# First 1024 tokens of a retention-plus-MLP kernel as 256-token pairs of sessions with a block-diagonal state product, and product 1's token sums on GpSimd

## The chip, the cores and the metric

One core of a Trainium2 chip. The metric is the device time of one execution in microseconds (us), the median over several executions.

The engines are named as in the profile: PE is TensorE's matmul side, PEld its weight loads, DVE is VectorE, ACT is ScalarE, POOL is GpSimd. "Bank" means one PSUM bank of 128 partitions by 512 fp32 columns.

## The reference

The reference is retention (a linear attention with decay, 8 batches, 8 heads, 576 positions, 64 per head) followed by an MLP on 4608 tokens with 512 inputs and 2048 hidden units, whose gate is h cos h:

```python
scores = scale * np.matmul(q, k.transpose(0, 1, 3, 2))
gamma = 1.0 - 2.0 ** (-5.0 - np.arange(H, dtype=np.float32))
Dmat = np.where(rel >= 0, gamma[:, None, None] ** rel[None, :, :], 0.0)
ret = scores * Dmat[None, :, :, :]
attn = np.matmul(ret, v)
# ... heads put side by side: x is (4608, 512)
h = x @ w_in                 # 512 -> 2048
g = h * np.cos(h)
out = g @ w_out              # 2048 -> 512
```

## The kernel before

The program lists its operations with the data that each reads and writes. When it is built, a list scheduler with a cost for each operation puts them in one fixed order per engine and gives each a PSUM bank.

Retention is computed in chunks with a running state. The first 1024 tokens go in 128-token sessions (token pairs share a partition), the rest in smaller pieces. One session does the scores, their mask, the product with the state so far (inter), the state update and the product with V (intra):

```python
def big_s(self, g):
    boxes, x, pt = [Box(), Box()], SES[g][0], self.PT[g % self.NPT]
    ...
    self.P.add("pe", mm, r=self.kkeys(g), w=boxes, cost=0.24 + 0.19)      # scores
    for hp in range(2):
        self.P.add("dve", mask(hp), r=boxes + ["trb"], ...)               # mask 128x512
```

V is scaled on 128 partitions and must then be shifted to the partitions where the session wants it:

```python
SHIFT = ('act', 'dve')
# cast_v, for the first eight tiles
for x in range(2):
    self.copy(SHIFT[x], ap(self.NAT[na], 2 * DM, 64 * x, 64, DM, [1, DM]),
              self.vt(t)[p0:p0 + 64, x * DM:(x + 1) * DM],
              [("sv", vb, x), ("sv", vb)], [("nat", na, 1, x)], DM, 0.75)
```

The state is copied from PSUM into a block-diagonal tile (two heads on the diagonal) by two 64-partition copies:

```python
for hp, eng in enumerate(engs):
    self.move(eng, lambda hp=hp: (
        ap(self.SBD[g % self.NSB], 1024, 64 * hp, 64, u0 * 512 + 64 * hp, [512, m], [128, 4], [1, 64]),
        ap(self.ST, 1024, 64 * hp, 64, u0 * 512, [512, m], [64, 4], [1, 64])), ...)
```

The first projection (mlp1) is a matmul group of 512 columns in one bank, a cosine on ACT, and on DVE the product of the two, which frees the bank and is called "the gt eviction" below:

```python
self.P.add("pe", mm, r=[("win", f // 2) for f in fs] + xts, w=[box], ...)
self.P.add("act", lambda e: e.activation(ap(cb, ...), self.bk(box.i, 0, 128, 0, m), AF.Sin, ...), ...)
self.P.add("dve", lambda e: e.tensor_tensor(ap(gt, ...), self.half_bank(box.i, ...), ap(cb, ...), ALU.mult), ...)
```

The second projection uses seven Strassen products per 512-token block. They need sums of gt halves ("token sums") and of w_out quarters ("weight sums"). All token sums are on DVE before the change. The sum for product 1 is

```python
self.P.add("dve", lambda e: e.tensor_tensor(
    ap(self.S1, HF * HB, 0, 128, f * HB, [HB, 2], [1, HB]), half(0, 0), half(1, 1), ALU.add), ...,
    cost=0.36, port=True, lazy=True)      # lazy: the scheduler takes it when nothing else is ready
```

## Time and profile before

| | before |
|---|---|
| time, median of 3 runs | 301.75 us (301.29 to 302.21) |
| span in the trace | 300.8 us |
| first useful projection matmul | 20.44 us |
| 8th, 16th, 24th gt eviction ended | 33.20, 42.77, 54.25 us |
| first Strassen product | 94.09 us |
| last matmul ended, last instruction ended | 297.75, 300.83 us |

How to read it: the span runs from the first to the last instruction. A line of a group has line number, engine, operation, output and inputs with their shapes, count, then busy time and mean ns of one, then the idle time just before them and who ended it. A line of waits has the engine and its output, who it waited for, then us in total, times and the longest. The lines themselves are in the prediction.

Two milestones: the first product, before which the front of the kernel lies, and the last matmul.

### The profile page before, as it was taken

The numbers are of one execution on the slowest core, as the hardware profiler recorded it, in microseconds if no ns is written. First come the engines' busy times: TensorE is split into PE (matmuls) and PEld (weight loads), VectorE is DVE, ScalarE is ACT, GpSimd is POOL, SyncE is SP. The second block draws the span as 40 slices with busy tenths as digits, with TensorE's granted clock in tenths as the row PEclk, the third lists the DMA queues.
The fourth block names the chain that finished last, engine by engine and source line by source line (L and its number), as shares of the span: only waits on it lengthen the run. The fifth ranks groups of instructions, "written<-read, shape, count | busy, mean of one in ns | idle before, by whom it ended". The sixth has DMA issues, their size and how long they took to land.

```text
span 300.8 us, 8802 instructions
## 1 busy us (share of the span) xinstructions
PE 288.0 (96%) x3659; PEld 206.2 (69%) x3695; DVE 239.5 (80%) x384; ACT 197.7 (66%) x340; POOL 143.7 (48%) x141
## 2 busy tenths in 40 slices
PE   8879899999999999999899999999999999999995
PEld 3457668765688885767576666676766676666684
DVE  5899889997899599679966985798589839964961
ACT  6467889946787556776667776766676767545420
POOL 4422950899854498088408941794050014002313
DMA  7999999899999999799859996999212011202023
GB/s 199 290 347 318 281 182 213 203 241 223 247 194 173 223 245 231 170 188 193 183 134 218 216 199 164 226 208 160 56 35 72 2 42 33 61 11 70 16 91 105
DMA packets 123894, 50.11 MB, mean 167 GB/s; under 512 B 82384, under 2 KB 123344, under 8 KB 123856
## 3 DMA queue, kind: packets, MB, share of 16 engines
q1 hardware_dynamic: 121744, 47.46, 74.4%
q0 software_dynamic: 2112, 2.10, 4.4%
q8 instruction: 29, 0.48, 0.7%
q14 instruction: 9, 0.07, 0.1%
HBM read 36.70 MB, written 9.44 MB: 153 GB/s over the span
## 4 chain that ended last, share of the span: by engine, by line
PE 80%; ACT 5%; DVE 4%; SPq 4%; DMA 3%; issue 2%; POOLq 0%; POOL 0%; DVEq 0%
PE bk L809 37%; PE bk L926 31%; PE bk L834 4%; DMA gt<-in_moe_w_in_dram 3%; ACT cb L817 2%; SPq L426 2%; PE st L640 2%; PE bk L619 2%; DVE gt L820 2%; PE bk L610 1%; PE bk L629 1%; SPq L445 1%; PE bk L567 1%; ACT xt L676 1%; ACT win L484 1%
## 5 line engine op out<-in xcount | busy, mean ns | idle before, releaser
L809 PE MATMUL bk<-xt,win 128*128 128x512 bf16 (+2 forms) x788 | 133.7, 314 | 4.2 <-DVE gt L820 1.0
L820 DVE TENSOR_TENSOR gt<-bk,cb 128x512 bf16<-128x512 f32 x144 | 95.9, 685 | 37.4 <-ACT cb L817 36.1
L817 ACT ACTIVATE cb<-bk,cpi 128x512 bf16<-128x512 f32 x144 | 97.8, 687 | 42.0 <-PE bk L809 37.3
L809 PEld LDWEIGHTS bk<-xt,win 128*128 128x128 bf16 x816 | 72.8, 98 | 41.1 <-ACT win L484 0.9
L961 POOL TENSOR_TENSOR sv<-sv,os 128x512 f32<-128x512 f32 x16 | 21.0, 1315 | 87.9 <-ACT os L970 66.7
L532 POOL TENSOR_TENSOR qnat<-qstg,wt 128x512 bf16<-128x512 f32 x34 | 38.9, 1164 | 19.2 <-DMA qstg<-in_q_dram 18.2
L676 ACT ACTIVATE sbd<-st 64x512 bf16<-64x512 f32 (+1 forms) x64 | 36.5, 570 | 15.0 <-PE bk L610 13.6
L487 POOL CAST nat<-stg 128x512 bf16<-128x512 f32 x36 | 27.3, 767 | 26.5 <-DMA stg<-in_k_dram 26.5
L522 POOL TENSOR_TENSOR nat<-stg,wt 128x512 bf16<-128x512 f32 x28 | 35.5, 1267 | 3.9 <-DMA stg<-in_v_dram 3.9
L926 PE MATMUL bk<-wout,gt 128*128 128x256 bf16 x256 | 31.7, 273 | 0.0
L926 PE MATMUL bk<-wout,s 128*128 128x256 bf16 x256 | 31.3, 273 | 0.3 <-DVE s L888 0.3
L926 PE MATMUL bk<-tw,gt 128*128 128x256 bf16 x256 | 31.3, 273 | 0.0
L676 ACT ACTIVATE xt<-bk 128x256 bf16<-128x256 f32 (+1 forms) x64 | 27.3, 488 | 5.4 <-DVE pt L655 3.8
L888 DVE TENSOR_TENSOR s<-gt 128x1024 bf16<-128x1024 bf16 x32 | 28.8, 902 | 1.4 <-PE bk L926 1.2
L926 PEld LDWEIGHTS bk<-wout,gt 128*128 128x128 bf16 x256 | 25.0, 98 | 6.1
L926 PEld LDWEIGHTS bk<-wout,s 128*128 128x128 bf16 x256 | 24.5, 98 | 6.4 <-DVE s L888 0.8
L895 DVE TENSOR_TENSOR gt<-gt 128x1024 bf16<-128x1024 bf16 x32 | 28.1, 881 | 0.0
L926 PEld LDWEIGHTS bk<-tw,gt 128*128 128x128 bf16 x256 | 24.0, 98 | 5.3 <-ACT sv L965 1.0
L655 DVE TENSOR_TENSOR pt<-bk,tri 128x512 bf16<-128x512 f32 (+2 forms) x30 | 19.8, 663 | 3.8 <-PE bk L610 3.7
L892 DVE TENSOR_TENSOR s<-gt 128x512 bf16<-128x512 bf16 x32 | 21.3, 664 | 0.0
L961 POOL TENSOR_TENSOR sv<-sv 128x512 f32<-128x512 f32 x8 | 13.2, 1656 | 15.5 <-ACT sv L965 10.3
L970 ACT ACTIVATE os<-bk 128x512 f32<-128x512 f32 x16 | 9.6, 597 | 13.0 <-PE bk L926 12.9
(75 smaller groups left out, 273.5 us busy)
## 6 DMA issues: line engine op xcount, KB each, us to landing
out_dram<-os SPq DMA_DIRECT2D x31, 256.0 KB, 2.4
qstg<-in_q_dram SPq DMA_DIRECT2D x12, 512.0 KB, 5.8
stg<-in_k_dram SPq DMA_DIRECT2D x24, 256.0 KB, 4.4
stg<-in_v_dram SPq DMA_DIRECT2D x24, 256.0 KB, 5.4
stg<-in_k_dram SPq DMA_DIRECT2D x4, 512.0 KB, 7.2
stg<-in_v_dram SPq DMA_DIRECT2D x4, 512.0 KB, 7.4
gt<-in_moe_w_in_dram SPq DMA_DIRECT2D x4, 512.0 KB, 8.5
wout<-in_moe_w_out_dram POOLq DMA_DIRECT2D x4, 512.0 KB, 10.8
```

What stands on the lines that cost most here:

```text
L487: self.P.add(eng, lambda e: e.tensor_copy(dst, src), r=r, w=w, cost=cost, port=eng == "pool")
L522: self.P.add(eng, lambda e: e.tensor_tensor(ap(self.NAT[na], 2 * DM, 0, 128, DM, [D, H], [1, D]), ap(self.STG[st], 2 * DM, 0, 128, DM, [D, ...
L532: self.P.add(eng, lambda e, x=x: e.tensor_tensor(ap(self.QNAT[slot], 2 * DM, 0, 128, x * DM, [D, H], [1, D]), ap(self.QSTG[slot], 2 * DM, ...
L676: self.P.add(eng, (lambda e: e.activation(*io(), AF.Copy)) if eng == "act" else (lambda e: e.tensor_copy(*io())), r=r, w=w, cost=0.127 + 0 ...
L809: inst = e.matmul(self.bk(box.i, 0, 128, i * n, n), ap(self.WIN, 4 * DFF, 0, 128, c * DFF + 128 * f, [1, 128]), ap(self.XT, 4 * XR, 0, 128 ...
L817: self.P.add("act", lambda e: e.activation(ap(cb, TB, 0, 128, 0, [1, m]), self.bk(box.i, 0, 128, 0, m), AF.Sin, bias=self.CPI.ap(), scale= ...
L820: self.P.add("dve", lambda e: e.tensor_tensor(ap(gt, NF * TB, 0, 128, f0 * TB + lo - TB * j, [TB, len(fs)], [1, n]), self.half_bank(box.i, ...
L888: self.P.add("dve", lambda e: e.tensor_tensor(ap(self.S5, HF * TB, 0, 128, f * TB, [1, 2 * TB]), ap(gt, NF * TB, 0, 128, f * TB, [1, 2 * TB]),
L892: self.P.add("dve", lambda e: e.tensor_tensor(ap(self.S1, HF * HB, 0, 128, f * HB, [HB, 2], [1, HB]), half(0, 0), half(1, 1), ALU.add), r= ...
L895: self.P.add("dve", lambda e: e.tensor_tensor(ap(gt, NF * TB, 0, 128, f * TB + HB, [HF * TB - HB, 2], [TB, 2], [1, HB]), ap(gt, NF * TB, 0 ...
L926: inst = e.matmul(self.bk(box.i, 0, 128, at * HB, HB), ap(lt, lsize, 0, 128, loff + f * lstep + 128 * t, [1, 128]), ap(rt, rsize, 0, 128, ...
L961: self.P.add(eng, lambda e: e.tensor_tensor(out(), a(), b(), op), r=r, w=w, cost=1.04 if eng == "pool" else 0.09 + 0.00104 * n * HB, port= ...
```

## The change

The intent: handle two sessions (256 tokens) together, so that V needs no shift, K is transposed and evicted for a pair at once, and the state is masked into its block-diagonal form by a single 128x512 product with a mask BD. With ACT relieved in the front, projections are woven through attention from the third unit on. In the later blocks, GpSimd adds the token sums of product 1. The last products are also re-ordered and held back differently. The diff, cut:

```diff
-HOLD = (2, 4)
-LS = (0, 1, 2, 3, 4, 5)
+HOLD = (1, 4)
+LS = (0, 1, 4, 2, 3, 5)
-EO, ES, EQ = ('act', 'act'), ('dve', 'dve'), ('pool', 'dve')
-WP = (7, 7, 7, 7, 8, 7, 7, 10)
-WC = ("dve", "act", "act", "dve", "pool", "dve", "dve", "act")
-G1, G2, WG = 3, 5, ("stg", 1, 1, 0)
-EARLY = 12
+EO, ES, EQ = ('act', 'act'), ('dve', 'act'), ('dve', 'pool')
+WP = (6, 5, 7, 8, 6, 9, 10, 9)
+WC = ("pool", "act", "act", "pool", "pool", "act", "act", "dve")
+G1, G2, WG = 3, 4, ("stg", 1, 1, 0)
+EARLY = 2
-SHIFT = ('act', 'dve')
-UNITS = ((0, 256, (0, 12)), (256, 512, (0, 12)), (0, 512, (12, 16)))
+UNITS = ((0, 256, (0, 10)), (256, 512, (0, 10)), (0, 512, (10, 16)))
+POOLED = 4
 ... (cast_v: the shift copies)
-            for x in range(2):
-                self.copy(SHIFT[x], ap(self.NAT[na], 2 * DM, 64 * x, 64, DM, [1, DM]),
-                          self.vt(t)[p0:p0 + 64, x * DM:(x + 1) * DM],
-                          [("sv", vb, x), ("sv", vb)], [("nat", na, 1, x)], DM, 0.75)
 ... (step_tk: one transpose group and one eviction of 128x1024 per pair; ev_st: one masked product)
+            self.P.add("dve", lambda e: e.tensor_tensor(
+                ap(self.SBD[g % self.NSB], 1024, 0, 128, u0 * 512, [128, 4], [64, 2], [1, 64]),
+                ap(self.ST, 1024, 0, 128, u0 * 512, [64, 4], [0, 2], [1, 64]),
+                ap(self.BD, 128, 0, 128, 0, [0, 4], [64, 2], [1, 64]), ALU.mult), ...)
 ... (big_s, big: scores, masks and intra products for two sessions at once, in 64-row tiles)
 ... (token_sums)
-        self.P.add("dve", lambda e: e.tensor_tensor(
+        eng = "pool" if j >= POOLED else "dve"
+        self.P.add(eng, lambda e: e.tensor_tensor(
             ap(self.S1, HF * HB, 0, 128, f * HB, [HB, 2], [1, HB]), half(0, 0), half(1, 1), ALU.add),
 ... (schedule)
-        run([m1(lo, hi, *fs) for lo, hi, fs in units[EARLY:]], [lambda: T(need[0])] + att_of(need[0], req(640)))
+        run([m1(lo, hi, *fs) for lo, hi, fs in units[EARLY:]], [lambda: T(need[0])] + att_of(need[0], need[0] + 2))
-        run([m1(512, 640, *f) for f in fours], att_of(req(640), req(768)))
-        run([m1(640, 768, *f) for f in fours], att_of(req(768), need[1]))
+        run([m1(512, 768, f, f + 1) for f in range(0, 16, 2)], att_of(need[0] + 2, need[1]))
```

WP spaces the loads of w_in among the other loads, WC says which engine casts each of its eight pieces, EARLY is the number of projection units issued ahead of any weaving, UNITS their shapes. LS is the order of the last products, HOLD how many products are held back, EO, ES and EQ the engines of some of attention's copies. A sum that moves to GpSimd also loses its `lazy` mark.

## The prediction

> **What bounds the kernel now.** I read the summary of the page first, then busy times by stage, then the tensor engine's waits in the stage that looked loose, then the groups that the change touches, and last the end of the chain. The summary and the slices of 7.5 us:
>
> ```profile
> PE 288.0 (96%) x3659; PEld 206.2 (69%) x3695; DVE 239.5 (80%) x384; ACT 197.7 (66%) x340; POOL 143.7 (48%) x141
> ...
> PE   8879899999999999999899999999999999999995
> ...
> DVE  5899889997899599679966985798589839964961
> ```
>
> TensorE (PE) bounds most of the span. 96% is no proof alone: a busy PE may run small matmuls badly. So I took the starts of successive matmuls in the timeline. From 94 us on, 128x512 matmuls follow each other every 216 ns and 128x256 ones every 109 ns, one moving column per 0.42 ns in both, and the weight loads (98 ns) hide. That pace does not improve; only holes can go. The table by stage (columns: window, its length, then busy us of PE, PEld, DVE, ACT, POOL) shows where they are:
>
> ```profile
> 20.40:54.50 34.10, 31.80 (x465) 25.15 (x468) 31.52 (x52) 29.26 (x47) 15.83 (x18) 1.00 1.13 252
> 54.50:94.30 39.80, 39.22 (x582) 29.54 (x585) 35.51 (x48) 29.72 (x55) 30.98 (x30) 1.00 1.10 219
> 94.30:294.30 200.00, 196.74 (x2427) 140.31 (x2453) 155.32 (x234) 127.40 (x222) 85.29 (x74) 1.00 0.67 133
> ```
>
> The first row runs from the first useful projection matmul to the moment when all projections of the first 768 tokens are issued. Counted by columns at full pace, its useful PE work is about 25 us of 34: some 9 us are holes or thin sequences. DVE is 92% and ACT 86% busy there, GpSimd only 46%. In the third row PE has 3.3 us of holes in 200 us. So the stage from 20 to 54 us is bound by evictions, by DVE before ACT, and by chains between them; the rest by PE. PE's waits from 18 to 62 us say whom it waits for:
>
> ```profile
> PE bk L695 <- DVE qt L541: 1.5, 2, 1.0
> PE bk L809 <- DVE gt L820: 0.6, 2, 0.4
> PE bk L809 <- ACT win L484: 0.6, 1, 0.6
> PE bk L809 <- DVE win L487: 0.4, 1, 0.4
> ```
>
> Each is an engine that was late because of its queue, none a DMA directly.
>
> **What the Trainium skill says.** "VectorE: DVE Perf Modes", section "The perf-mode tier table", gives a two-tensor operation with a PSUM operand the 1x rate and a copy from PSUM at most 2x. The trace agrees: 512 fp32 columns from PSUM take 685 ns in the cosine product, 1024 bf16 columns copied from PSUM 686 ns (groups below). Hence a masked product of 128x512 is not cheap. "SBUF — State Buffer", section "Who interferes with whom", says that a DVE instruction with two SBUF inputs contends with GpSimd reads, and one with a single SBUF input outside the two-port modes does not. The trace agrees sharply: the token sum that the change moves takes 407 to 1495 ns, the PSUM product 673 to 693 ns. "GPSIMD Engine Reference", section "Elementwise — side-by-side cycle accounting", has GpSimd 1.96 times slower than DVE on a two-tensor add; here its bf16-giving 128x512 product takes about 1.05 us (V scaling) against 0.41 undisturbed for the DVE sum. "TensorEngine Tiling (Array Packing)", section "PSUM Bottleneck", warns that after tiling the PSUM copies may become the bottleneck. That is this stage.
>
> ```profile
> L820 DVE TENSOR_TENSOR gt<-bk,cb 128x512 bf16<-128x512 f32 x144 | 95.9, 685 | 37.4 <-ACT cb L817 36.1 <-PE bk L610 0.5
> L892 DVE TENSOR_TENSOR s<-gt 128x512 bf16<-128x512 bf16 x32 | 21.3, 664 | 0.0
> L540 ACT ACTIVATE kt<-bk 128x512 bf16<-128x512 bf16 x14 | 8.1, 594 | 3.3 <-PE bk L549 3.2
> L541 DVE COPY qt<-bk 128x1024 bf16<-128x1024 bf16 x8 | 5.5, 686 | 1.0 <-PE bk L567 0.9
> L484 ACT ACTIVATE nat<-sv 64x512 bf16<-64x512 bf16 x8 | 5.0, 625 | 3.9 <-DVE sv L511 3.8
> L487 DVE COPY nat<-sv 64x512 bf16<-64x512 bf16 x8 | 3.6, 450 | 0.2
> L676 DVE CAST sbd<-st 64x256 bf16<-64x256 f32 x8 | 3.3, 418 | 0.2
> L676 ACT ACTIVATE sbd<-st 64x256 bf16<-64x256 f32 x6 | 2.2, 371 | 0.1
> ```
>
> **The change part by part, first 1024 tokens.** *PE work*: per 256 tokens the scores go from 16 matmuls of 64x128 to 32 of 64x64, and the intra products likewise from 16 to 32. Before two such tiles share the array, after four do, so the columns streamed per time stay equal: 8 x 56 ns = 0.45 us each, as the 16 score matmuls show now (0.62 us from first start to last end, with 0.17 of latency). I take zero change. The 512-to-768 projections become 64 matmuls at 109 ns in place of 128 at 56 ns: 0.2 us less.
>
> *Removed*: the V shifts, 8 x 0.625 = 5.0 us of ACT and 8 x 0.450 = 3.6 us of DVE; the half-size state copies, 3.3 us of DVE and 2.2 of ACT; eight K evictions of ACT, 4.8 us. *Added*: seven masked state products of 0.61 to 0.69 us on DVE, 4.5 us; four paired K evictions, 4 x 0.69 = 2.7 us of DVE. V scaling (4 DVE operations, 3.2 us) and two more weight casts go to GpSimd; three DVE weight casts vanish, ACT gets one more and the early K casts.
>
> For the stage 20.4 to 54.5 alone, by what falls in it: DVE loses 1.8 (shifts), 1.5 (state) and about 1.5 (casts), and gains five masked products, 3.0, and two K evictions, 1.4: a net of -0.4. It also contains 1.5 us of weight sums that need not be there. Its compulsory work is thus 31.5 - 1.5 - 0.4 = 29.6 us, an estimate. ACT goes from 29.3 to about 25. So ACT leaves the bound, while DVE hardly sheds work; what improves is the chain. Session 3 now finishes 6 us after the scores of its pair because state copy, inter product, state and intra follow one another per session; after, the scores of 256 tokens are masked at once and the intra products need no shift. The new load order also brings the second pair of sessions' inputs two loads earlier (some 1.9 us each), and attention is woven through the projections from the third unit on.
>
> The first projection can start when its weights are cast: they stay eighth in the queue, and a GpSimd cast no longer waits behind four DVE masks; I allow 0.8 us. From 19.6, 29.6 us of DVE without a hole gives 49.2; a little over 1 us of holes gives 50.3. That is 4.2 us before the 54.5 of now.
>
> *Next stage (54.5 to 94.3)*: the 1.5 us of weight sums return, and six more K evictions move from ACT to DVE at about 0.4 us (half of the 686 ns copy and some start cost), 2.4 us. DVE would go from 35.5 to 39.4 of 39.8 us. It can't hide wholly: I add 0.8 us.
>
> *Token sums*: 20 of the 32 sums go to GpSimd, 20 x 0.66 = 13.3 us off DVE. But PE waits only once for a token sum after 120 us, 0.3 us, with a hole near 206 us that a late DVE queue caused. I give 0.5 us, no more: DVE's idle time in a PE-bound stage costs nothing.
>
> *End*: the last matmul is at 297.75 and the result leaves DVE 0.6 us later. The chain shows GpSimd in between:
>
> ```profile
> 294.29 0.61 ACT sv L965
> 294.90 0.07 issue
> 294.97 1.27 POOL sv L961
> 296.23 0.04 issue
> 296.28 1.32 POOLq L1166
> ```
>
> GpSimd's second subtraction ends at 297.6, as PE does; making product 1 earlier removes GpSimd from the chain but PE's end stays. 0.3 us.
>
> The sum: -4.2 + 0.8 - 0.5 - 0.3 = -4.2, rounded with the 0.2 us of projections to -4.4: 301.75 - 4.4 = 297.4.
>
> **Rivals.** *PSUM banks become the bound.* A pair of sessions holds two output banks from the first inter product to the last intra, beside two or four for scores, of six. That leaves two for projections that each hold one for some 2.6 us (0.86 PE, 0.69 ACT, 0.69 DVE, latencies). For it: these holds lie in the very stage where the gain is sought. Against it: there are only two such pairs after the first projections. It would cost 1 to 3 us, for 298.5 to 300.5. *DVE saturates and gives it all back.* For it: 39.4 of 39.8 us above, and more contention now that GpSimd does more. Then 300 to 302. *The front runs as PE would allow.* Of the 9 us of holes, 8 go, and the second stage keeps its pace: 292.5 to 294.5. For it: ACT is freed, GpSimd half idle, loads better interleaved. Against it: DVE's 29.6 us does not fit under 26 us of PE work. *GpSimd's sums come late for product 1*: half a microsecond per block at most, five blocks, 2.5 us worse; the product is fifth of seven, so I hold it unlikely.
>
> **Range and chances.** Front gains of 1 to 8 us, and returns of 0 to 2 us, give 293.5 to 301.5. 2% is 6.0 us, a time under 295.7: that needs nearly the whole front, 0.31. Slower by 2% needs two rivals at once, 0.05. Within 2%: 0.64.
>
> **What would show it.** Right: the projections of the first 768 tokens end near 50 us; shifts are gone; ACT is near 25 us in that stage and DVE near full; from 94 us to the end the length is within 1 us of before, with DVE some 12 us less busy. Wrong: PE waits on PSUM releases by DVE around the paired sessions (banks), or PE holes between 50 and 90 us behind DVE, or product 1 waiting for GpSimd. If the front ends before 47 us I have overrated DVE as its bound; if the third stage shrinks by more than 1.5 us I have underrated the sums.

## The result, and the profile after

| | before | after |
|---|---|---|
| time, median | 301.89 us (301.29 to 302.21, 4 runs) | 299.99 us (299.62 to 300.22, 4 runs) |
| span in the trace | 300.8 us | 297.8 us |
| first useful projection matmul | 20.44 us | 16.31 us |
| 8th, 16th, 24th gt eviction ended | 33.20, 42.77, 54.25 us | 35.00, 43.29, 54.09 us |
| first Strassen product | 94.09 us | 91.92 us |
| last matmul ended | 297.75 us | 295.33 us |
| last matmul to last instruction | 3.08 us | 2.51 us |

The ratio is 0.9938, 95% interval 0.9919 to 0.9957: the change gains 1.9 us. A repeat of the same kernel in other rounds gave 0.9926, a gain of 2.2 us. A ratio here is the mean time of one kernel's fast runs over that of the other's in the same rounds, so it is not quite the ratio of the medians. Executions over 1.5% slower than the fastest of the same kernel are left out of the means. The two traces differ by 3.0 us because the profiled execution of before was about 0.5 us above the median span of its kernel (300.3) and that of after about 0.3 us below (298.1).

The summary of after and its slices of 7.4 us:

```profile
PE 289.4 (97%) x3751; PEld 204.2 (69%) x3751; DVE 230.9 (78%) x369; ACT 186.8 (63%) x317; POOL 172.7 (58%) x166
...
PE   8988899999999998999999999999999999999996
...
DVE  5775899999799299669957995799589738964961
```

The table by stage in the same three windows (window, its length, then busy us of PE, PEld, DVE, ACT, POOL):

```profile
20.40:54.50 34.10, 30.79 (x465) 22.90 (x465) 28.85 (x47) 23.84 (x36) 17.40 (x21) 1.00 1.15 254
54.50:94.30 39.80, 39.80 (x627) 29.99 (x628) 36.53 (x58) 26.38 (x48) 32.60 (x31) 1.00 1.14 224
94.30:294.30 200.00, 199.17 (x2440) 140.62 (x2426) 150.35 (x216) 126.57 (x220) 111.84 (x95) 1.00 0.61 132
```

In the first row ACT fell from 29.26 to 23.84 us and DVE from 31.52 to 28.85, and yet PE is *less* busy there (30.79 against 31.80). The front has lost its evictions' load without filling PE.

One trap in these tables: the trace of before has 3659 matmuls against 3695 weight loads, while after has 3751 of each. Some 36 matmul records of before are missing. A part of what looks like more PE work after (199.17 against 196.74 in the third row) is only complete records. I therefore counted PE afresh from the starts of all matmuls, with the missing ones put back beside their weight loads. It is my own count: useful columns at full pace; waits, which are gaps over 0.15 us; the rest, which are the short gaps, mostly between small tiled matmuls.

```
window      before: useful  waits  rest     after: useful  waits  rest
16 to 32            10.9    3.0    1.3              9.8    4.0    1.5
32 to 41             6.7    1.8    0.5              8.1    0.2    0.7
41 to 54            10.5    0.7    1.9             11.1    0.7    1.2
54 to 62             7.6    0.4    0.1              7.7    0.0    0.3
62 to 92            27.5    0.0    2.5             27.9    0.0    2.1
92 to 150           54.0    1.0    3.0             53.9    1.2    3.0
150 to 290         134.2    0.5    5.3            134.5    0.0    5.5
```

(The first row also holds warm-up matmuls: 0.9 us before, 0.6 us after.) The lead of after over before, in useful PE work done since the start of the trace, is 1.5 us at 54 us, 2.2 us at 92 us and 2.4 us at 290 us.

The waits of PE from 18 to 62 us in after:

```profile
PE bk L704 <- DVE gt L855: 0.8, 1, 0.8
PE bk L844 <- ACT win L491: 0.7, 1, 0.7
PE bk L844 <- DVE gt L855: 0.7, 2, 0.5
PE bk L844 <- POOL win L494: 0.6, 1, 0.6
```

L704 are the scores of a pair. They wait for gt evictions, whose banks they need. The two "win" waits are for casts of w_in. The scores' 1.5 us of waits for the eviction of transposed Q (the largest before) are gone.

The groups that the change adds or moves, by shape:

```profile
L712 DVE TENSOR_TENSOR pt<-bk,trb 128x512 bf16<-128x512 f32 x16 | 10.1, 680 | 1.9 <-PE bk L704 1.9
L667 DVE TENSOR_TENSOR sbd<-st,bd 128x512 bf16<-128x512 f32 x7 | 4.8, 680 | 0.7 <-PE bk L763 0.7
L928 POOL TENSOR_TENSOR s<-gt 128x512 bf16<-128x512 bf16 x20 | 28.3, 1422 | 13.4 <-DVE gt L855 13.4
L932 DVE TENSOR_TENSOR gt<-gt 128x1024 bf16<-128x1024 bf16 x32 | 33.0, 1035 | 0.2
L923 DVE TENSOR_TENSOR s<-gt 128x1024 bf16<-128x1024 bf16 x32 | 30.7, 969 | 3.1 <-PE bk L963 2.8
```

The masked products cost what the prediction gave them (680 ns). A sum on GpSimd takes 1422 ns, and the two kinds of sums left on DVE became slower than before: 1035 against 881 ns and 969 against 902. That is 32 x 0.154 + 32 x 0.067 = 7.1 us of the 13.3 us taken off DVE given back. DVE fell only from 155.32 to 150.35 us in the third stage, where the prediction had some 12. The slowing follows the move: the changed kernel without it (a_nopool below) has these sums at 823 and 867 ns, and the kernel before with it (b_pool) at 999 and 988 ns. Net, the move takes 3.3 us off DVE in this stage (150.35 us against 153.63 in a_nopool), not 13.3.

The end of the chain of waits (start, us, what):

```profile
274.43 5.18 PE bk L844 x24
279.61 15.73 PE bk L963 x144
295.36 0.42 DVE os L998
```

GpSimd is no longer in it.

### The profile page after: what moved, and what is told of

Same layout as the page of the kernel before. It is cut to its first block, busy times and chain, and to the rows that moved or that the text cites. A ratio compares the mean times of both kernels' runs of the same rounds, so it can differ in the third digit from the quotient of the medians.

```text
span 297.8 us, 8942 instructions
## 1 busy us (share of the span) xinstructions
PE 289.4 (97%) x3751; PEld 204.2 (69%) x3751; DVE 230.9 (78%) x369; ACT 186.8 (63%) x317; POOL 172.7 (58%) x166
## 4 chain that ended last, share of the span: by engine, by line
PE 85%; DVE 5%; SPq 4%; DMA 3%; ACT 1%; issue 1%; DVEq 0%
PE bk L844 39%; PE bk L963 32%; PE bk L869 5%; DMA gt<-in_moe_w_in_dram 3%; PE st L638 2%; SPq L433 2%; PE bk L617 2%; SPq L466 1%; DVE gt L855 1%; PE bk L608 1%; PE bk L627 1%; PE bk L565 1%; SPq L452 1%; DVE s L923 1%; PE bk L552 1%
## 5 line engine op out<-in xcount | busy, mean ns | idle before, releaser
L844 PE MATMUL bk<-xt,win 128*128 128x512 bf16 (+1 forms) x744 | 138.9, 331 | 2.8 <-ACT win L491 0.7
L844 PEld LDWEIGHTS bk<-xt,win 128*128 128x128 bf16 x744 | 70.9, 98 | 43.7 <-issue 1.0
L532 POOL TENSOR_TENSOR qnat<-qstg,wt 128x512 bf16<-128x512 f32 x34 | 39.9, 1191 | 20.1 <-DMA qstg<-in_q_dram 20.1
L680 ACT ACTIVATE sbd<-st 64x512 bf16<-64x512 f32 x58 | 34.3, 592 | 12.0 <-PE bk L608 10.5
L494 POOL CAST nat<-stg 128x512 bf16<-128x512 f32 x32 | 24.7, 776 | 20.5 <-DMA stg<-in_k_dram 15.9
L928 POOL TENSOR_TENSOR s<-gt 128x512 bf16<-128x512 bf16 x20 | 28.3, 1422 | 13.4 <-DVE gt L855 13.4
L522 POOL TENSOR_TENSOR nat<-stg,wt 128x512 bf16<-128x512 f32 x28 | 32.5, 1161 | 1.9 <-DMA stg<-in_v_dram 1.7
L932 DVE TENSOR_TENSOR gt<-gt 128x1024 bf16<-128x1024 bf16 x32 | 33.0, 1035 | 0.2
L923 DVE TENSOR_TENSOR s<-gt 128x1024 bf16<-128x1024 bf16 x32 | 30.7, 969 | 3.1 <-PE bk L963 2.8
L653 DVE TENSOR_TENSOR pt<-bk,tri 128x256 bf16<-128x256 f32 (+3 forms) x39 | 20.4, 543 | 1.5 <-PE bk L608 1.3
```

The lines of the kernel that those rows point to most:

```text
L494: self.P.add(eng, lambda e: e.tensor_copy(dst, src), r=r, w=w, cost=cost, port=eng == "pool" or half == 0.75)
L522: self.P.add(eng, lambda e: e.tensor_tensor(ap(self.NAT[na], 2 * DM, 0, 128, DM, [D, H], [1, D]), ap(self.STG[st], 2 * DM, 0, 128, DM, [D, ...
L532: self.P.add(eng, lambda e, x=x: e.tensor_tensor(ap(self.QNAT[slot], 2 * DM, 0, 128, x * DM, [D, H], [1, D]), ap(self.QSTG[slot], 2 * DM, ...
L680: self.P.add(eng, (lambda e: e.activation(*io(), AF.Copy)) if eng == "act" else (lambda e: e.tensor_copy(*io())), r=r, w=w, cost=0.175 + 0 ...
L844: inst = e.matmul(self.bk(box.i, 0, 128, i * n, n), ap(self.WIN, 4 * DFF, 0, 128, c * DFF + 128 * f, [1, 128]), ap(self.XT, 4 * XR, 0, 128 ...
L923: self.P.add("dve", lambda e: e.tensor_tensor(ap(self.S5, HF * TB, 0, 128, f * TB, [1, 2 * TB]), ap(gt, NF * TB, 0, 128, f * TB, [1, 2 * TB]),
```

## The experiments

My theory after the first look: the front was tied by chains through evictions and banks, not by the volume of any engine, so freeing ACT and DVE paid only where the order of work could use it. The rivals: DVE's volume (the prediction's own step), the three cosine tiles, the arrival of weights, and, for the rest of the kernel, the token sums.

### Does the pair layout or the interleaving make the front's gain?

**a_front**: the changed kernel with the old settings of the front.

```diff
-WP = (6, 5, 7, 8, 6, 9, 10, 9)
-WC = ("pool", "act", "act", "pool", "pool", "act", "act", "dve")
-EARLY = 2
-UNITS = ((0, 256, (0, 10)), (256, 512, (0, 10)), (0, 512, (10, 16)))
+WP = (7, 7, 7, 7, 8, 7, 7, 10)
+WC = ("dve", "act", "act", "dve", "pool", "dve", "dve", "act")
+EARLY = 12
+UNITS = ((0, 256, (0, 12)), (256, 512, (0, 12)), (0, 512, (12, 16)))
```

> The changed kernel with the old order of weight loads and casts, the old split of the first projections and twelve of them early (the retuning of the front undone, the new session structure kept). If the structure alone brings the gain: within 0.7 us of the changed kernel. If the interleaving is needed to cash it: 1 to 3 us longer. The prediction laid most of the gain on the chain and the interleaving together.

Measured: 302.14 us (301.65 to 304.13), ratio to before 1.0004 (0.9960 to 1.0048). The whole gain is gone, and the first product starts at 94.33 us, as before (94.09). The first projection starts at 21.30 us (16.31 in after), and PE's longest waits from 16 to 62 us are 1.6 us each, for a gt eviction and for a cast of w_in. The run undoes load order, cast engines and interleaving together, so it doesn't say which of them counts.

**b_front**: the reverse, the kernel before with the new settings and order, its shifts and single sessions kept.

```diff
-WP = (7, 7, 7, 7, 8, 7, 7, 10)
+WP = (6, 5, 7, 8, 6, 9, 10, 9)
 ... (WC, G2, UNITS likewise)
-EARLY = 12
+EARLY = 2
-        run([m1(512, 640, *f) for f in fours], att_of(req(640), req(768)))
-        run([m1(640, 768, *f) for f in fours], att_of(req(768), need[1]))
+        run([m1(512, 768, f, f + 1) for f in range(0, 16, 2)], att_of(need[0] + 2, need[1]))
```

> The kernel before with the changed kernel's order of work alone: its load spacing, its weight-cast engines, projections from the third unit on woven through attention, 256-wide projections of tokens 512 to 768. The V shifts, the half-size state copies and the single-session blocks stay. If the interleaving makes the front gain and the pair layout only enables room for it, this is 1.5 to 2.2 us below the kernel before (ratio 0.993 to 0.995). If the pair layout with its freed scalar engine is needed as well (my theory), the tensor engine waits for score masks and shifted V in the front, and the time is at the kernel before or up to 2 us above it (ratio 1.000 to 1.007).

Measured: 306.77 us (306.41 to 307.59), ratio 1.0159 (1.0142 to 1.0176): 4.7 us slower than before, a larger loss than either theory had. The longest of PE's waits from 41 to 92 us:

```profile
PE bk L610 <- DVE gt L820: 1.8, 1, 1.8
```

And the row of its table by stage around it:

```profile
60.00:66.00 6.00, 3.51 (x33) 2.53 (x32) 5.79 (x11) 2.52 (x4) 5.39 (x6) 0.84 0.94 232
```

Scores waited 1.8 us for a gt eviction, PE was busy for 3.5 of 6 us while DVE was busy for 5.8, and the granted clock fell to 0.84 in that stretch. All four runs have a mean clock of 0.994, and the trace has half clock from 64.08 to 67.50 us, so up to 1.7 us of the loss (an estimate: half of 3.41) may be the clock's. Both halves are needed as they stand: the new order is worth nothing without the pair layout and costs 4.7 us, and the pair layout without the order is worth nothing. (Both runs change several settings at once, and neither was fitted to its layout. A better order for either may exist.)

### Is DVE's volume the bound of the front?

**a_nomask**: the sixteen score masks cut to 8 of their 512 columns. The result is wrong, and the order of all queues is otherwise unchanged.

```diff
-                    ap(pt, 1024, 0, 128, hp * 512, [256, 2], [1, 256]),
+                    ap(pt, 1024, 0, 128, hp * 512, [256, 2], [1, 4]),
 ... (the two inputs likewise; two GpSimd memsets fill the tile beforehand)
```

> The changed kernel with each of the 16 score masks of the first 1024 tokens cut to 8 columns of 512 (wrong result on purpose, every order kept): about 0.55 us less each on DVE, 6.6 us of it between 16 and 54 us. Volume (the prediction's step: the front is as long as DVE's compulsory work): 4 us faster or more. Chain (only the tensor engine's waits behind DVE count, 2 to 3 us of them between 16 and 54 us): 1.5 to 3 us faster. If loads alone set the front: under 0.7 us.

Measured: the fast runs took 298.58 to 299.46 us, ratio 0.9885 (0.9848 to 0.9921), 1.2 to 1.6 us below the changed kernel by its two ratios (0.9926 and 0.9938). The profiled execution fell into a state of 591.7 us, with matmuls at half pace throughout, so its trace was of no use.

**a_nomask2**: the same kernel, for a trace.

> The kernel with the sixteen score masks cut to 8 of 512 columns once more, for a usable trace (the first one fell in an abnormal state of twice the time; its result is wrong on purpose). If the vector engine's volume bounded the front, as my prediction's step had it, the 16 masks less take 5 us or more off the 16 to 54 us stage. If the chain does, the tensor engine's waits in 16 to 32 us fall by 1.5 us at the most, and the vector engine's idle time grows by most of the 6 us taken from it.

Measured: 298.67 us, one run (state unknown). Its table by stage, below that of after in the same windows:

```profile
16.00:32.00 16.00, 13.11 (x237) 9.77 (x235) 10.38 (x18) 9.49 (x13) 9.96 (x11) 1.00 1.14 325
32.00:41.00 9.00, 8.77 (x106) 5.32 (x107) 8.38 (x15) 6.66 (x11) 7.64 (x10) 1.00 1.17 233
41.00:54.00 13.00, 12.62 (x191) 9.97 (x190) 12.60 (x21) 9.41 (x17) 2.50 (x3) 1.00 1.16 210
```

```profile
16.00:32.00 16.00, 13.60 (x242) 10.39 (x242) 8.56 (x19) 10.08 (x14) 10.11 (x11) 1.00 1.14 324
32.00:41.00 9.00, 8.69 (x105) 5.02 (x103) 7.03 (x15) 6.64 (x11) 7.65 (x10) 1.00 1.16 234
41.00:54.00 13.00, 12.78 (x196) 10.50 (x195) 10.96 (x21) 9.52 (x16) 2.48 (x4) 1.00 1.16 207
```

DVE's busy time from 16 to 54 us fell by 1.8 + 1.4 + 1.6 = 4.8 us. What became of it is in DVE's waits of that stretch, first after, then this run:

```profile
DVE gt L855 <- ACT cb L852: 3.4, 5, 1.7
```

```profile
DVE gt L857 <- ACT cb L854: 7.7, 10, 1.7
```

DVE waits 4.3 us longer for cosines, and PE's useful work is 0.8 us ahead at 54 us. Nine tenths of the DVE time set free became DVE idling, a sixth became PE's gain (the two overlap). The prediction's "DVE's compulsory work" did not set the length.

**a_nostate**: the seven masked state products cut to 8 of 512 columns (wrong).

```diff
-                ap(self.SBD[g % self.NSB], 1024, 0, 128, u0 * 512, [128, 4], [64, 2], [1, 64]),
+                ap(self.SBD[g % self.NSB], 1024, 0, 128, u0 * 512, [128, 4], [64, 2], [1, 1]),
 ... (the two inputs likewise)
```

> The changed kernel with the seven masked state products cut to 8 columns of 512 (wrong result on purpose, order kept): 0.55 us less each, 2.8 us of DVE between 16 and 54 us, and a shorter link between a session's state and the next one's inter product. If what the change put on DVE in place of the half-size state copies is the cost that the prediction had too small: 1.5 to 3 us faster. If not: under 1 us.

Measured: 299.58 us (298.94 to 300.23), ratio 0.9911 (0.9872 to 0.9951). No clear difference from the changed kernel (0.9926 and 0.9938).

**a_dve**: the opposite, six more DVE operations (memsets of 128x768, 0.70 us each by its trace) in the front.

```diff
+            for x in range(2 if 0 < t and t % 2 == 0 else 0):
+                self.P.add("dve", lambda e: e.memset(self.SCR.ap(), 0.0),
+                           r=[("stg", st, y, p) for y in range(2) for p in (0, 64)], w=["scr"], cost=0.0)
```

> The changed kernel with six extra DVE memsets of 128x768 fp32 (some 0.7 us each, 4.4 us in all: about what the change took off DVE between 16 and 41 us), two after each of the second, third and fourth pairs of sessions are loaded; they write a scratch tile that nobody reads, and the order of everything else is unchanged. Theory L: DVE has slack there, so under 1 us longer. Theory D: nearly all of it shows, 3 to 4.4 us longer.

Measured: 302.33 us (301.08 to 304.58), ratio 0.9996 (0.9974 to 1.0018): 1.8 to 2.1 us behind the changed kernel by its two ratios, of 4.2 us added. But the profiled run (304.58) had a stretch of half clock, which the other five had not. Their mean alone is 302.15 us, 1.4 to 1.7 us behind. So added DVE work costs 0.3 to 0.4 of itself, and removed DVE work gives a sixth back. That fits a chain of which DVE is one link, and not a bound by DVE's volume.

### Is it the cosine tiles?

In after, a projection issued at 26.6 us got its cosine only at 32.05 us and held its bank for about 8 us, and the tile that its cosine needed had been freed late. So I gave it six tiles instead of three and pinned everything else: the scheduler plans with three, and the tiles are renamed afterwards, so that the order of all engines and all banks are the same (I compared them).

**a_cb6pin**:

```diff
-        self.NPT, self.NSB, self.NCB, self.NOS = 2, 2, 3, 4
+        self.NPT, self.NSB, self.NCB, self.NOS = 2, 2, 6, 4
 ... (planned with n_cb % 3, waits worked out with n_cb % 6)
```

> The changed kernel with six cosine tiles in place of three, the instruction order of every engine and all PSUM banks kept exactly. If the 4.0 us of waits between 16 and 32 us rest on the three cosine tiles (the scalar engine cannot start a cosine before the vector engine has read the tile's last one), those waits fall by 1 us or more and the time with them (ratio to before 0.988 to 0.990). If the fixed order of the vector engine's queue and the six PSUM banks make them, nothing moves (0.991 to 0.994, as the changed kernel).

Measured: 299.91 us (299.25 to 302.11), ratio 0.9936 (0.9911 to 0.9961), PE's largest waits from 16 to 32 us unchanged (0.8 for a gt eviction, 0.7 and 0.6 for casts). The edit did take effect: ACT's waits for gt evictions from 16 to 41 us, 2.6 us in after, were gone. The cosine tiles are not the cause. What is left of this explanation, the fixed order of ACT's and DVE's queues over the six banks, could not be tried alone: the program holds six banks and two more for the state, I had none to add, and another order is another plan.

### Is it the arrival of the weights?

**a_halfw**: weight loads of half the bytes (wrong), the same casts.

```diff
-            ap(t, size, 0, 128, 2048 * i, [512, 4], [1, 512]).bitcast(F32),
+            ap(t, size, 0, 128, 2048 * i, [512, 2], [1, 512]).bitcast(F32),
 ... (the source likewise; the cast reads the half twice)
```

> The changed kernel, but each of the eight loads of the first projection's weights brings half its bytes (2.1 MB less in all), and the cast reads the loaded half twice: a wrong result on purpose; the order of instructions on PE, ACT, DVE and GpSimd is the same. Theory L (the first 41 us of the changed kernel are paced by the arrival of loads, about 10.5 MB at some 290 GB/s, so freeing DVE and ACT bought little): 2.1 MB less is 7 us of stream less, and the time falls by 3 to 5 us, to 295 to 297. Theory D of the prediction (DVE's volume or the chains between engines set the front): the time falls by less than 1 us.

Measured: 306.14 us, ratio 1.0136 (1.0112 to 1.0161): slower with less to load. The timeline of DVE (start, us, engine, what) says why:

```profile
30.71 4.95 DVE L494 CAST win<-tw 128x1024 bf16<-128x1024 f32 x1
```

And the table by stage, just after it:

```profile
35.00:42.00 7.00, 5.68 (x18) 2.72 (x19) 5.54 (x9) 2.66 (x4) 2.16 (x3) 0.51 1.20 205
```

A cast of 128x1024 on DVE, for which the groups of after have 0.68 us, took 4.95 us, while GpSimd ran two casts and then four products, one behind the other without a pause from 30.91 us on (until 36.56). The cast's new read pattern is not the reason: in b_halfw DVE's casts with it took 0.69 to 1.04 us. PE waited 4.34 us behind it, and from 35 to 42 us the granted clock was 0.51. The Trainium skill, page "SBUF — State Buffer", section "Who interferes with whom", says that a DVE copy or cast can enter a mode in which it contends with GpSimd and that the loser "fully blocks (not throttle)". This trace agrees, and shows that the loser can miss its turn over several instructions. Page "TensorE: Matmul & The Clock Gate", Part 1, has the clock at half after an idle window of about 3.4 us. The trace agrees: PE idled 32.0 to 36.3 us, and half clock lasted two periods of 3.41 us, 35.14 to 41.97. But other traces show that no whole idle window is needed: in b_front PE was busy for 1.55 us of the 3.41 us before its period of half clock, with no pause over 1.8 us. So this run answers another question than the one asked.

**b_halfw**: the same edit in the kernel before.

> The same halving of the weight loads in the kernel before; a wrong result on purpose. Theory L with DVE close behind (DVE 92% busy in the front of the kernel before): falls too, but by less than in the changed kernel, 1 to 3 us. If the kernel before was bound by DVE alone in its front: under 0.5 us. If loads bound it alone: as much as in the changed kernel.

Measured: 305.86 us (303.6 to 307.62), ratio 1.0115 (1.0073 to 1.0156), with the same accident: two copies of DVE took 2.98 us, and a period of half clock followed. Inconclusive for the same reason.

**a_wc**: the control for a clean repeat, the changed kernel with its last weight cast on ACT, out of GpSimd's way. It was re-planned, so its queues differ from those of the changed kernel; a_halfw2 has exactly its order.

```diff
-WC = ("pool", "act", "act", "pool", "pool", "act", "act", "dve")
+WC = ("pool", "act", "act", "pool", "pool", "act", "act", "act")
```

> The changed kernel with the last weight cast on ACT in place of DVE. It is the control of the next run: a DVE cast between two SBUF tiles was locked out for 4.95 us by GpSimd in the first try with half the weight bytes. Both theories: within 1 us of the changed kernel.

Measured: 299.59 us (298.65 to 300.59), ratio 0.9916 (0.9886 to 0.9946), as the changed kernel within its interval.

**a_halfw2**: a_wc with half the weight bytes.

> The control with half the bytes in each weight load (wrong result on purpose), every engine's order as in the control. Theory L (loads pace the tensor engine's waits between 16 and 32 us, some 1.6 us of the 4.0 by the casts that came late, and DVE's idle time there): 1.5 to 3 us faster than the control, with the waits for weight casts gone. Theory D (DVE's chain and PSUM releases pace it): within 0.7 us of the control.

Measured: 298.87 us (298.04 to 298.95), ratio 0.9884 (0.9854 to 0.9915), 0.7 us by the medians and 1.0 us by the ratios below its control (299.59, 0.9916), though the intervals overlap. Waits of PE from 16 to 32 us fell from 4.4 to 3.2 us. So about 1 us goes away when half of the weights' bytes need not be loaded. What the other half costs, no run shows.

**a_again**: the changed kernel unaltered, for these rounds.

> The changed kernel itself, as the yardstick on this chip: ratio to the kernel before 0.992 to 0.996, as first measured (0.9938).

Measured: 299.84 us (299.61 to 300.26), ratio 0.9926 (0.9904 to 0.9949).

### What are the token sums worth?

**a_nopool**: the changed kernel with all token sums on DVE, re-planned.

```diff
-POOLED = 4
+POOLED = 99
```

> The changed kernel with all token sums on DVE (the GpSimd part undone). The prediction gave it 0.5 us: 0.3 to 0.7 us longer than the changed kernel, if PE seldom waits for DVE after 120 us. A rival in which the sums carry most of the measured gain: 1.5 us longer or more. A rival in which GpSimd's sums cost as much as they give: no difference, within 0.2 us.

Measured: 301.69 us (300.70 to 302.58), ratio 0.9978 (0.9957 to 0.9998), 1.2 to 1.6 us behind the changed kernel by its two ratios. The first product starts at 92.02 us, as in after, and the last matmul ends 2.2 us later, in a profiled run that was its slowest (302.58). The tail after it is 3.03 us against 2.51, so 0.5 us of the loss lies there.

**b_pool**: the same sums moved in the kernel before, re-planned as well.

```diff
+        eng = "pool" if j >= 4 else "dve"
-        self.P.add("dve", lambda e: e.tensor_tensor(
+        self.P.add(eng, lambda e: e.tensor_tensor(
             ap(self.S1, HF * HB, 0, 128, f * HB, [HB, 2], [1, HB]), half(0, 0), half(1, 1), ALU.add),
```

> The kernel before with the GpSimd part alone: product 1's token sums of blocks 4 to 8 on GpSimd. If the part gives in the kernel before what undoing it cost the changed kernel (1.2 us), 300.7 or 0.4% faster. If it can only remove the waits that the kernel before had after 92 us (1.5 us by its trace, two of three near DVE's late sums): 0.5 to 1.2 us faster. The prediction's figure: 0.5 us.

Measured: 302.07 us, ratio 0.9998 (0.9973 to 1.0022). Worth nothing there.

**a_nopool_h2**: a_nopool with the old holding rule of the products, `HOLD = (2, 4)`, in case the new rule is what needs the sums elsewhere.

> The changed kernel without the move of the token sums, re-planned, with the old holding rule of the last products (2, 4 in place of 1, 4). If the earlier run without the move lost its 1.2 to 1.6 us because the new rule needs the sums on GpSimd, this is back at the changed kernel (0.991 to 0.994 of before). If the sums on the vector engine cost it by themselves, it stays at 0.997 to 0.999.

Measured: 301.70 us (300.82 to 302.13), ratio 0.9984 (0.9966 to 1.0001), the same as a_nopool. The rule is not it.

**a_sums_dve**: the sums back on DVE with every other queue pinned. After planning, the twenty operations are handed from GpSimd to DVE at their place in the plan. I compared the orders: PE and ACT are unchanged, DVE and GpSimd changed by these operations alone.

```diff
+        for op in self.ops:
+            if any(k[0] == "s1" for k in op.w if isinstance(k, tuple)):
+                op.eng = "dve"
         self.settle()
```

> The changed kernel with product 1's 20 late token sums given back to the vector engine at the same place in the program, every other engine's order kept exactly (the earlier run without the move re-planned all queues). If the move itself is worth the 1.2 to 1.6 us that the re-planned run lost, this loses about as much against the changed kernel (ratio to before 0.997 to 0.999). If that loss came from the re-planned order, this equals the changed kernel (0.991 to 0.994), as my prediction's half microsecond would have it.

Measured: 305.46 us (304.93 to 306.11), ratio 1.0111 (1.0094 to 1.0128): 5.5 us worse than the changed kernel, far over both expectations. The group of the sums on DVE from 92 to 292 us, and PE's longest waits from 150 us to the end:

```profile
L931 DVE TENSOR_TENSOR s<-gt 128x512 bf16<-128x512 bf16 x28 | 20.8, 741 | 0.0
```

```profile
PE bk L847 <- DVE gt L858: 1.2, 3, 0.9
PE bk L620 <- DVE gt L858: 1.1, 2, 0.7
PE bk L847 <- ACT xt L683: 0.9, 1, 0.9
```

After has no PE wait over 0.15 us there. DVE is busy 157.85 us from 92 to 292 us, against 151.98 in after and 157.51 in before: the same load as before, with 42 us idle, and still the kernel loses 5.5 us. So what a sum on DVE costs hangs on where it stands in the queue. In this plan it stands where GpSimd was to take it, with no `lazy` mark, and PE waits for gt evictions; the kernel before, whose sums are `lazy` fillers on DVE, gains nothing by giving them away (b_pool). Re-planning recovers about 4 us of the 5.5.

### The shorter tail

**a_ls**: the changed kernel with the old order of the last products.

```diff
-LS = (0, 1, 4, 2, 3, 5)
+LS = (0, 1, 2, 3, 4, 5)
```

> The changed kernel with the old order of products in the last block. One look at the end: from the end of the last matmul to the last instruction, 3.1 us as in the kernel before, against 2.5 us in the changed one, if the order of products is the cause; 2.5 us if it is not.

Measured: 300.32 us, one run. From the last matmul's end to the last instruction it takes 3.08 us, as before (3.08), against 2.51 after. The order makes the shorter tail. It isn't enough by itself: a_nopool and a_nopool_h2, which keep the new order but were re-planned, show 3.03 us each.

### A version meant to beat both

**a_knobs**: the changed kernel with settings found by trying a few hundred in its own scheduler and taking the plan it thought shortest.

```diff
-WP = (6, 5, 7, 8, 6, 9, 10, 9)
-WC = ("pool", "act", "act", "pool", "pool", "act", "act", "dve")
-EARLY = 2
-UNITS = ((0, 256, (0, 10)), (256, 512, (0, 10)), (0, 512, (10, 16)))
-FILL, SLOW = 24.0, 5.6
-POOLED = 4
+WP = (4, 5, 7, 8, 6, 9, 10, 9)
+WC = ("pool", "act", "act", "act", "pool", "act", "act", "act")
+EARLY = 4
+UNITS = ((0, 256, (0, 12)), (256, 512, (0, 12)), (0, 512, (12, 16)))
+FILL, SLOW = 18.0, 5.6
+POOLED = 3
 ... (and five cosine tiles)
```

> A version meant to beat both kernels: the changed kernel with other front settings (first two weight loads spaced 4 and 5 instead of 6 and 5, two casts moved to the scalar engine, four projection units ahead of attention instead of two, 256-wide projections for 12 instead of 10 tiles, product 1's sums on GpSimd from block 3, five cosine tiles). If the loads' order is what is left to be had in the front, it gains 0.5 to 1.2 us on the changed kernel (ratio to before 0.988 to 0.991). If the remaining waits are a matter of queues and banks that move elsewhere with each setting, it is within 0.5 us of the changed kernel (0.992 to 0.995).

Measured: 298.72 us (298.48 to 298.90), correct, ratio 0.9882 (0.9865 to 0.9899): 3.6 us below before, and below the changed kernel by 1.1 us in the medians (299.84 in its repeat) and 1.3 to 1.7 us by the ratios. Not for the reason that I gave, though: its first product starts at 91.89 us (91.92 in after), its waits from 16 to 32 us are 3.4 us, and its lead over after, 0.65 us in the trace, arises between 110 and 150 us, in the blocks where GpSimd now also takes the sums of block 3 (POOLED = 3) and where PE's waits fell from 1.2 to 0.5 us. (FILL and the cosine tiles changed too, so this isn't isolated.) The rest of the timed gain lies in which runs were profiled: its profiled span (297.2) is 0.3 us above its median (296.9), that of after 0.3 us below.

## Why the prediction was right or wrong

*The direction and parts of the mechanism* held. ACT left the bound of the front (predicted near 25 us, measured 23.84), the shifts are gone, the masked products cost 680 ns, the new order is needed (a_front) and GpSimd left the end of the chain. From the first product to the last instruction the length stayed within 1 us (206.7 and 205.9 us), as expected; DVE's load there fell by 5 us instead of some 12: the term "20 x 0.66 = 13.3 us off DVE" left out that the sums that stay on DVE become slower, as shown above.

*The size* did not: 4.4 us predicted, 1.9 measured (2.2 in the repeat). By the prediction's own sum, from the traces:

| term | predicted | measured |
|---|---|---|
| front, next stage, narrower projections, up to the first product | -4.2 + 0.8 - 0.2 = -3.6 | 91.92 - 94.09 = -2.17 |
| token sums, first product to last matmul | -0.5 | 203.41 - 203.66 = -0.25 |
| tail | -0.3 | 2.51 - 3.08 = -0.57 |

(The measured column adds to 3.0, the difference of the two traces; the timed medians differ by 1.9 to 2.2, as told above.)

*The step that failed* is the front: "Its compulsory work is thus 31.5 - 1.5 - 0.4 = 29.6 us", and "From 19.6, 29.6 us of DVE without a hole gives 49.2; a little over 1 us of holes gives 50.3." It took DVE's volume as what sets the length. The volume came out as predicted, even a little lower (28.85 us from 20.4 to 54.5), but DVE stood idle for 5.2 of these 34.1 us, where the prediction allowed a little over 1. So the 24th gt eviction ended at 54.09 us instead of near 50, although the first projection started at 16.31 us, earlier than the 19.6 predicted. And a_nomask2 took 4.8 us of DVE's volume away, of which PE gained 0.8. The step before it failed with it: "some 9 us are holes or thin sequences". Counted from matmul starts, before has from 16 to 54 us 5.5 us of waits and 3.7 us of short gaps, and the short gaps stayed (3.4 us after); both kernels do their attention in small tiles. Page "TensorEngine Tiling (Array Packing)", section "Key Properties", states that changing the tiling mode drains TensorE. No run here isolates that, but gaps that stay with the tiles fit it. So 5.5 us could be had at most, not 9, and of them the change got 0.6 (4.9 us of waits remain in 16 to 54 us), because waits from 16 to 32 us grew from 3.0 to 4.0 us while those of 32 to 41 us nearly vanished. The rest of the lead at 54 us is work done before 16 us, and fewer short gaps and warm-up matmuls.

*The next stage* was predicted 0.8 us worse, with DVE at 39.4 of 39.8 us. It was 36.53, and the stage ran 0.7 us better (lead 1.5 us at 54, 2.2 at 92). The step counted DVE work added and not the waits that earlier work had left behind.

*What bounds 16 to 32 us now* is partly open. About 1 us goes with half of the weights' bytes (a_halfw2), nothing with the cosine tiles (a_cb6pin), 0.8 us up to 54 us with DVE's masks (a_nomask2, whose gain may overlap). For the rest, the waits in the trace and the program say that ACT, DVE and PE wait for one another in turn: scores wait for the bank of a projection, whose gt eviction waits for a cosine, which stands behind other work in ACT's queue. That is argued, not shown: no experiment could change banks or one queue alone.

*The token sums* came out at half of the predicted size in the sum (-0.25), and that is luck. "DVE's idle time in a PE-bound stage costs nothing" doesn't hold in general, as a_sums_dve shows: at the same places in the plan, the sums on DVE cost 5.5 us with 42 us of DVE idle. Nor is the move worth 0.5: it is worth 0 in the kernel before and 1.2 to 1.6 in the changed one, 0.5 of it in the tail. Why a re-planned kernel without the move loses that much in one and nothing in the other stays open. The holding rule is excluded (a_nopool_h2), and chance in the plans is not. Without the move, most of the front's gain would not have reached the end.

*The rivals.* "PSUM banks become the bound" is the nearest: its 298.5 to 300.5 holds the result, and the scores' 0.8 us wait on a gt eviction is its sign, but the waits are spread over four causes. "DVE saturates" did not happen (36.53 of 39.8 us). "The front runs as PE would allow" was far off. Of what was to show the prediction wrong, "PE holes between 50 and 90 us behind DVE" did not show, and "PE waits on PSUM releases by DVE around the paired sessions" did.

## What to carry to other kernels

An engine that is 92% busy beside a waiting PE is not yet its bound: before working out a gain from its volume, look at what it waits for itself, and count PE's waits from matmul starts, separate from short gaps that go with the tiles. A structure that frees engines and an order that uses them may each be worth nothing or less alone, so try both together, and in a kernel whose plan is computed, pin the plan when you test one operation. An operation's cost on an engine with idle time depends on what stands behind it in that queue.

## What the Trainium skill lacked or had wrong

- "SBUF — State Buffer", section "Who interferes with whom", says that the loser of the shared port blocks for the whole instruction of the other. Here a DVE cast of 128x1024, 0.68 us otherwise, took 4.95 us across five successive GpSimd instructions (a_halfw). The page doesn't say that successive instructions can keep the port.
- "GPSIMD Engine Reference", section "Elementwise — side-by-side cycle accounting", has GpSimd 1.96 times slower on a two-tensor add, for 2048 fp32 elements; it has no ratio for bf16. Here the 128x512 bf16 sum takes 1422 ns on GpSimd in company, against 407 ns for the fastest on DVE and 664 ns for the mean on DVE before, 3.5 and 2.1 times. The slowing of DVE's own sums by it (881 to 1035 and 902 to 969 ns) has no figure there.
- "TensorEngine Tiling (Array Packing)", section "Key Properties", gives no figure for the change of tiling mode. Short gaps around the small tiles add to 3.4 to 3.7 us from 16 to 54 us here; no run shows how much of them is the drain.
- "TensorE: Matmul & The Clock Gate", Part 1, gives no share of busy time below which the clock halves. Here PE was busy for 1.55, 1.64 and 1.69 us of the 3.41 us before a period of half clock (b_front, a_dve, a_knobs). These runs do not settle the share.
- No page has a figure for what order alone is worth: with the same 20 sums on DVE, one plan takes 4 us longer than another (a_sums_dve against a_nopool).
